# Load order and first row tiles of a layernorm + attention + SwiGLU kernel: weight pieces issued ahead of x, and transposes split over two PSUM banks

## The chip, the cores and the metric

The kernel runs on one core of one Trainium2 chip. The metric is the time of one execution on the device, in microseconds (us). Executions of one kernel mostly differ by 0.8 to 1.8 us; so single executions are read through their profiles, of which there is one per run, and times only as medians and means of five or more.

The engines are TensorE (PE in the profile), VectorE (DVE), ScalarE (ACT), GpSimd (POOL) and SyncE (SP, which here issues most transfers). "SPq" is the sequencer of SyncE.

## The reference, cut to what matters

```python
x  = A_x                                   # 2048 x 640, bf16
xn = layernorm(x)                          # over the 640 columns
s  = attention(xn @ wq, last 512 of K and V, 32 heads of 192) @ wo
g  = silu((silu(xn @ w_gate) * (xn @ w_up)) @ w_down)     # hidden width 1536
return x + s * g
```

The kernel starts with the FFN. For that it needs the normalised x transposed (640 as five blocks of 128 partitions, `xnT`) and the weights w_gate and w_up. Only the first 512 rows, four tiles of 128 rows that are called tile 0 to tile 3 here, and their x that is called x0 to x3, are in the reach of the change.

## The kernel before: the parts that matter

The loads are issued in program order. The first quarter of the columns of each weight comes in three pieces: block 0, blocks 1 and 2, blocks 3 and 4 ("first", "second" and "third piece").

```python
load_x(0)                                   # two halves: SyncE and ACT
load_x(1, nc.scalar)
for cs in (slice(0, 1), slice(1, 3), slice(3, NC)):      # NC = 5 blocks
    if cs.stop == NC:
        load_x(2)
    for eng, w_sb, w in ((nc.sync, wg_sb, B_w_gate), (nc.scalar, wu_sb, B_w_up)):
        ...
        eng.dma_start(out=w_sb[:, cs, 0:FQ], in_=src)
load_x(3)
```

Each tile goes through statistics (DVE), a Sqrt (ACT), reciprocal and normalisation (DVE), five transposes into PSUM (TensorE), a copy to `xnT` (ACT; for tile 0 ACT and DVE) and 30 matmuls of 128 columns (TensorE). The next tile is prepared in the middle of the current one:

```python
for t in range(4):
    order = [(*fs, [c]) for c in range(NC) for fs in banks]   # block by block
    if t:
        order = [(*fs, range(NC)) for fs in banks]            # all five blocks at once
    for k, (f, s, cs) in enumerate(order):
        if k == len(order) * 3 // 5 and t < 3:
            if t == 1:
                ln_stats(3, lambda: ln_apply(2))   # DVE: half of x3's statistics, then tile 2's normalisation
            else:
                ln_apply(t + 1)
            ready(t + 1)                           # transposes and copy of the next tile
            if t == 0:
                ln_stats(2)
            ...
        hidden_mm(first[f][s][:, rows], s, f, rows, cs)
```

After these four tiles the FFN goes on with matmuls of 512 columns. "The start of the 512-wide matmuls" is therefore the moment at which the start-up is over.

The softmax here doesn't subtract the row's maximum and nothing guards it: scores larger than these inputs give would overflow.

Of the kernel before, what the change touches and what calls it, by code (L numbers as in the profile page):

```python
# [15 lines left out]
def kernel(  # L16
# [13 lines left out]
    nc = tc.nc  # L30
    P = nc.NUM_PARTITIONS

    x2 = A_x.flatten_outer_dims()
# [9 lines left out]
    NC = D // P  # L43
# [27 lines left out]
    def sc_tile():  # L71
        return psum.tile([P, 2, 512], f32, name="sc", tag="sc")

    def mm_tile():
        return psum.tile([P, 2, 512], f32, name="mm", tag="mm")
# [4 lines left out]
    xnT = res.tile([P, NC, Sq], bf, name="xnT")  # L80
# [3 lines left out]
    ident = consts.tile([P, P], bf, name="ident")  # L84
# [62 lines left out]
    lo, hi = slice(0, 64), slice(64, 128)  # L147
# [17 lines left out]
    with ExitStack() as fctx:  # L165
# [6 lines left out]
        zero_t = ffw.tile([P, 512], bf, name="zero_t")  # L172
        nc.vector.memset(zero_t[:], 0.0)
        wg_sb = ffw.tile([P, NC, F], bf, name="wg_sb")
        wu_sb = ffw.tile([P, NC, F], bf, name="wu_sb")
        wd_sb = ffw.tile([P, NF, D], bf, name="wd_sb")
        FQ = F // 4
        x_t, ln, xns = {}, {}, {}

        def load_x(t, eng=nc.sync):  # L180
            x_t[t] = lnx.tile([P, D], bf, name="x_t")
            if t == 0:
                for r, eng in ((lo, nc.sync), (hi, nc.scalar)):
                    eng.dma_start(out=x_t[t][r, :], in_=x2[t * P + r.start : t * P + r.stop, :])
            else:
                eng.dma_start(out=x_t[t][:], in_=x2[t * P : (t + 1) * P, :])

        def load_gu(q):
            cols = slice(q * FQ, (q + 1) * FQ)
            nc.sync.dma_start(  # L190
                out=wg_sb[:, :, cols], in_=B_w_gate[:, cols].rearrange("(c p) f -> p c f", p=P)
            )
            nc.sync.dma_start(
                out=wu_sb[:, :, cols], in_=B_w_up[:, cols].rearrange("(c p) f -> p c f", p=P)
            )

        load_x(0)
        load_x(1, nc.scalar)
        for cs in (slice(0, 1), slice(1, 3), slice(3, NC)):
            if cs.stop == NC:  # L200
                load_x(2)
            for eng, w_sb, w in ((nc.sync, wg_sb, B_w_gate), (nc.scalar, wu_sb, B_w_up)):
                src = w[cs.start * P : cs.stop * P, 0:FQ].rearrange("(c p) f -> p c f", p=P)
                eng.dma_start(out=w_sb[:, cs, 0:FQ], in_=src)
        load_x(3)
        load_gu(1)
        for t in range(4, 8):
# [6 lines left out]
        nc.scalar.activation(act_t[:], one_t[:], ACT.Sqrt)  # L214
        warm = sc_tile()

        def keep_warm(n):
            for _ in range(n):
                nc.tensor.matmul(warm[:, 0, :], zero_t[:, 0:P], zero_t[:], start=True, stop=True)

        keep_warm(11)

        def ln_stats(t, between=None):
            b, ti = divmod(t, 4)
            if ti == 0:
                ln[b] = [lnw.tile([P, 4, 2], f32, name="mv"), lnw.tile([P, 4], f32, name="rstd")]
            stats = lnw.tile([P, ng, nc.vector.BN_STATS_DIM], f32, name="stats")
            for g in range(ng):
                nc.vector.bn_stats(stats[:, g, :], x_t[t][:, g * (D // ng) : (g + 1) * (D // ng)])
                if g == 0 and between:  # L230
                    between()
            nc.vector.bn_aggr(ln[b][0][:, ti, :], stats[:])
# [7 lines left out]
        def ln_sqrt(t):  # L240
            mv, rstd = ln[0]
            nc.scalar.activation(
                rstd[:, t : t + 1], mv[:, t, 1:2], ACT.Sqrt, bias=eps_t[:], scale=1.0
            )

        def ln_apply(t, parts=(slice(0, D),)):
            b, ti = divmod(t, 4)
            mv, rstd = ln[b]
            xns[t] = lnx.tile([P, D], bf, name="xn", bufs=4)
            if b == 0:  # L250
                nc.vector.reciprocal(rstd[:, t : t + 1], rstd[:, t : t + 1])
            for cols in parts:
                nc.vector.tensor_scalar(
                    xns[t][:, cols], x_t[t][:, cols], mv[:, ti, 0:1], rstd[:, ti : ti + 1],
                    op0=ALU.subtract, op1=ALU.mult,
                )

        tps = {}

        def ln_transpose(t):  # L260
            xn = xns.pop(t)
            tps[t] = tp[:, t % 2, 0 : NC * P].rearrange("p (c k) -> p c k", c=NC)
            for c in range(NC):
                nc.tensor.transpose(tps[t][:, c, :], xn[:, c * P : (c + 1) * P], ident[:])

        def ln_transpose_dma(t):
            nc.sync.dma_start_transpose(
# [5 lines left out]
        def hidden_mm(out, s, f, qc, cs=range(NC)):  # L273
            w_sb = (wg_sb, wu_sb)[s]
            for c in cs:
                nc.tensor.matmul(  # L276
                    out, w_sb[:, c, f * P : (f + 1) * P], xnT[:, c, qc],
                    start=(c == 0), stop=(c == NC - 1),
                )

        def hidden_gate(b, f, g, u):
            sg = ffa.tile([P, 512], bf, name="sg")
            nc.scalar.activation(sg[:], g, ACT.Silu)  # L283
            nc.vector.tensor_tensor(hTs[b][:, f, :], u, sg[:], ALU.mult)  # L284
# [35 lines left out]
        first = {f: [sc[:, s, :] for s in range(2)] for f, sc in ((0, sc_tile()), (1, sc_tile()))}  # L320
        tp = psum.tile([P, 2, 1024], bf, name="tp", tag="mm")
        first[2] = [mm[:, s, :] for mm in (mm_tile(),) for s in range(2)]
        def ready(t):
            ln_transpose(t)
            rows = slice(t * P, (t + 1) * P)
            n = NC if t else 2
            nc.scalar.copy(xnT[:, 0:n, rows], tps[t][:, 0:n, :])
            if n < NC:
                nc.vector.tensor_copy(out=xnT[:, n:NC, rows], in_=tps[t][:, n:NC, :])

        ln_stats(0)
        ln_sqrt(0)
        ln_stats(1, lambda: ln_apply(0, (slice(0, 2 * P), slice(2 * P, D))))
        ready(0)
        ln_sqrt(1)
        keep_warm(3)
        banks = [(f, s) for f in range(3) for s in range(2)]
        for t in range(4):
            rows = slice(t * P, (t + 1) * P)

            order = [(*fs, [c]) for c in range(NC) for fs in banks]
            if t:
                order = [(*fs, range(NC)) for fs in banks]
            for k, (f, s, cs) in enumerate(order):
                if k == len(order) * 3 // 5 and t < 3:
                    if t == 1:
                        ln_stats(3, lambda: ln_apply(2))
                    else:
                        ln_apply(t + 1)
                    ready(t + 1)  # L350
                    if t == 0:
                        ln_stats(2)
                    if t < 2:
                        ln_sqrt(t + 2)
                    else:
                        nc.scalar.activation(act_t[:], one_t[:], ACT.Silu)
                hidden_mm(first[f][s][:, rows], s, f, rows, cs)
                if t == 3 and s == 1:
                    hidden_gate(0, f, *first[f])
# [394 lines left out]
```

## Time and profile before

| | before |
|---|---|
| median of 6 executions | 927.25 us (926.93 to 928.28) |
| span of the profiled execution | 925.4 us |
| first real matmul | 6.89 us |
| statistics of x2 start (DVE) | 8.09 us |
| transposes of tile 2 start (TensorE) | 10.55 us |
| 512-wide matmuls start | 15.56 us |

The page's first part gives for each engine its busy time, its share of the span and its instructions:

```profile
PE 917.3 (99%) x11085; PEld 624.9 (68%) x11101; DVE 575.6 (62%) x844; ACT 473.8 (51%) x847; POOL 100.1 (11%) x387
```

TensorE is busy for all but 8 us of the span, and part of these 8 us lies in the start, which is why a change there has so little to win. The last two rows of the table come from the timeline of TensorE (start, duration, line, operation, output and input, shapes, count):

```profile
10.55 0.45 PE L264 MATMUL tp<-ident,xn 128*128 128x128 bf16 x5
...
15.56 1.24 PE L276 MATMUL mm<-xnT,wg_sb 128*128 128x512 bf16 x4
```

The transposes of tile 2 have no idle time noted: before, tile 2 came just in time.

### The profile page before, as it was taken

To read this page: it belongs to the slowest core of one execution; us is meant where nothing else is said; L and a number is where in the kernel's file an instruction comes from. 1 tells how busy PE (TensorE), PEld (TensorE's weight loads), DVE (VectorE), ACT (ScalarE), POOL (GpSimd) and SP (SyncE) were. 2 spreads that over 40 slices of the span, in tenths; PEclk is the share of its full clock that TensorE was granted. 3 is DMA by queue.
4 is the path that set the end of the run, shared out by engine and by line. 5 is a ranking of instruction groups with operands and counts; after the bars stand their busy time and mean duration, and the time that the engine had idled before them with its cause. 6 is when DMAs were issued, how large, how long until landed. Compare 5 with 4: busy or idle time off the path is not lost.

```text
span 925.4 us, 25770 instructions
## 1 busy us (share of the span) xinstructions
PE 917.3 (99%) x11085; PEld 624.9 (68%) x11101; DVE 575.6 (62%) x844; ACT 473.8 (51%) x847; POOL 100.1 (11%) x387
## 2 busy tenths in 40 slices
PE   9999999999999999999999999999999999999997
PEld 5455556575858585868686867676767777776665
DVE  6433331467676767676766667676767676767655
ACT  4222222556464646565555565656555555556561
POOL 0000000000000000000000000000000000002976
PEclk9999999999999999999999999999999999999999
DMA  9321510044544445444536262536362717162624
GB/s 298 72 56 33 114 35 1 1 77 89 87 79 83 83 80 86 75 90 70 95 60 106 59 107 55 111 53 113 46 119 42 124 36 129 36 129 76 135 57 140
DMA packets 243810, 77.18 MB, mean 83 GB/s; under 512 B 224624, under 2 KB 243696, under 8 KB 243696
## 3 DMA queue, kind: packets, MB, share of 16 engines
q1 hardware_dynamic: 242640, 74.72, 41.5%
q8 instruction: 87, 1.43, 0.7%
q10 hardware_dynamic: 1056, 0.82, 0.3%
q14 instruction: 27, 0.22, 0.1%
HBM read 39.45 MB, written 2.62 MB: 45 GB/s over the span
## 4 chain that ended last, share of the span: by engine, by line
PE 98%; DMA 1%; DVE 0%; issue 0%; ACT 0%; DVEq 0%
PE mm L428 22%; PE sc L563 19%; PE sc L442 18%; PE mm L468 16%; PE sc L276 11%; PE mm L298 6%; PE sc L537 3%; PE mm L520 2%; DMA wg_sb<-in_B_w_gate_dram 1%; PE mm L276 0%; PE mm L311 0%; DMA OT_b<-O_b 0%; PE sc L520 0%; DMA x_t<-in_A_x_dram 0%; DVE s_f L638 0%
## 5 line engine op out<-in xcount | busy, mean ns | idle before, releaser
L446 ACT ACTIVATE p_t<-sc 128x1024 bf16<-128x1024 f32 x254 | 253.0, 1022 | 130.5 <-PE sc L442 130.5
L433 DVE TENSOR_REDUCE qT<-mm 128x512 bf16<-128x1024 f32 x189 | 231.2, 1223 | 104.8 <-PE mm L428 102.4
L498 ACT ACTIVATE O_b<-mm,r 128x192 bf16<-128x192 f32 x486 | 164.6, 421 | 183.1 <-issue 159.9
L428 PE MATMUL mm<-xnT,wq_p 64*128 64x512 bf16 x1890 | 237.7, 377 | 0.0
L563 PE MATMUL sc<-wo_p,OT_b 64*128 64x320 bf16 x2592 | 217.4, 296 | 0.5 <-DMA OT_b<-O_b 0.5
L588 DVE TENSOR_TENSOR sacc<-sacc,sc 128x640 f32<-128x640 f32 x200 | 164.1, 821 | 78.3 <-PE sc L563 78.3
L442 PE MATMUL sc<-qT,khat 64*128 64x512 bf16 x1524 | 198.3, 377 | 0.0
L468 PE MATMUL mm<-V_p,p_t 64*128 64x193 bf16 x3520 | 186.4, 243 | 0.0
L468 PEld LDWEIGHTS <-p_t 64*128 64x128 bf16 x3584 | 162.6, 94 | 12.0
L428 PEld LDWEIGHTS <-wq_p 64*128 64x128 bf16 x1890 | 105.6, 94 | 96.0 <-issue 0.5
L563 PEld LDWEIGHTS <-OT_b 64*128 64x128 bf16 x2592 | 139.9, 94 | 22.7 <-DMA OT_b<-O_b 1.1
L442 PEld LDWEIGHTS <-khat 64*128 64x128 bf16 x1536 | 85.6, 94 | 79.2 <-issue 2.9
L551 POOL MEMSET turn_t<- 128x1 f32 x328 | 32.2, 98 | 697.9 <-PE mm L468 474.6
L284 DVE TENSOR_TENSOR hT<-sc,sg 128x512 bf16<-128x512 f32 x46 | 31.7, 690 | 85.2 <-ACT sg L283 85.1
L283 ACT ACTIVATE sg<-sc 128x512 bf16<-128x512 f32 x46 | 27.3, 596 | 72.4 <-PE sc L276 72.4
L276 PE MATMUL sc<-xnT,wg_sb 128*128 128x512 bf16 (+1 forms) x248 | 58.6, 354 | 1.0 <-DMA wg_sb<-in_B_w_gate_dram 0.4
L276 PE MATMUL sc<-xnT,wu_sb 128*128 128x512 bf16 (+1 forms) x259 | 59.1, 355 | 0.1
L298 PE MATMUL mm<-wd_sb,hT 128*128 128x320 bf16 x384 | 56.6, 300 | 0.0
L487 DVE RECIPROCAL r<-mm 128x4 f32<-128x4 f32 x124 | 22.7, 183 | 48.1 <-PE mm L468 36.3
L298 PEld LDWEIGHTS <-hT 128*128 128x128 bf16 x384 | 37.5, 98 | 18.9
L276 PEld LDWEIGHTS <-wu_sb 128*128 128x128 bf16 x285 | 26.3, 98 | 26.9
L276 PEld LDWEIGHTS <-wg_sb 128*128 128x128 bf16 x285 | 26.3, 98 | 23.5 <-DMA wg_sb<-in_B_w_gate_dram 0.5
(67 smaller groups left out, 373.1 us busy)
## 6 DMA issues: line engine op xcount, KB each, us to landing
wo_p<-in_A_wo_dram SPq DMA_DIRECT2D x16, 480.0 KB, 4.6
K_p<-in_A_k_cache_dram SPq DMA_DIRECT2D x32, 192.0 KB, 3.4
V_p<-in_A_v_cache_dram SPq DMA_DIRECT2D x32, 192.0 KB, 3.0
wq_p<-in_A_wq_dram SPq DMA_DIRECT2D x64, 80.0 KB, 3.1
wq_p<-in_A_wq_dram SPq DMA_DIRECT2D x16, 160.0 KB, 3.5
x_r<-in_A_x_dram SPq DMA_DIRECT2D x16, 160.0 KB, 3.9
x_t<-in_A_x_dram SPq DMA_DIRECT2D x14, 160.0 KB, 3.0
OT_b<-O_b SPq DMA_TRANSPOSE x124, 2.8
```

Source lines behind the costliest of these rows:

```text
L276: nc.tensor.matmul(out, w_sb[:, c, f * P : (f + 1) * P], xnT[:, c, qc], start=(c == 0), stop=(c == NC - 1),)
L284: nc.vector.tensor_tensor(hTs[b][:, f, :], u, sg[:], ALU.mult)
L298: nc.tensor.matmul(dn[:, 0:HD], hTs[b][:, f, ti * P : (ti + 1) * P], wd_sb[:, f, cols], start=(f == 0), stop=(f == NF - 1),)
L428: nc.tensor.matmul(q_ps[:, h, :], pairs[pr]["wq"][r, c, j * P : (j + 1) * P], xnT[r, c, b * 512 : (b + 1) * 512], start=(c == 0), stop=(c ...
L433: nc.vector.reduce_sum(qTs[i][:, j, :], q_ps[:, :, :].rearrange("p h n -> p n h"), axis=AX.X)
L442: nc.tensor.matmul(sc[:, h, :], khat[r, j, ks], qT[r, j, :], start=(j == 0), stop=(j == 2))
L446: nc.scalar.activation(p_t[:, :, :], sc[:, :, :], ACT.Exp, scale=scale)
L468: m = nc.tensor.matmul(acc[:, k, h * 256 : h * 256 + Dh + 1], Ps[i][kc][r, h, qt * P : (qt + 1) * P], V_p[r, kc, h, 0 : Dh + 1], start=(p ...
L498: nc.scalar.activation(O_b[:, qt, h, :], a_k[:, h, 0:Dh], ACT.Copy, scale=r[:, k, h, :])
L551: st["turn"] = nc.gpsimd.memset(turn_t[:], 0.0)
L563: m = nc.tensor.matmul(ps[:, n, 0:HD], OTs[i][r, 3 * qt + j, :], pairs[i // NB]["wo"][r, j, n * HD : (n + 1) * HD], start=(turn == 0 and j ...
L588: nc.vector.tensor_tensor(s_t, s_t, sc[:, :, 0:HD], ALU.add)
```

## The change

Its intent: tile 0 needs the weight pieces soon and x1 and x2 later, so the pieces should go ahead. ACT should issue fewer transfers, so that its Sqrt table is loaded before it is needed. Transposes into two banks should let a copy begin while the other bank is still written. The warm-up matmuls, which only keep TensorE's clock up, should not delay the transposes.

```diff
         load_x(0)
-        load_x(1, nc.scalar)
-        for cs in (slice(0, 1), slice(1, 3), slice(3, NC)):
-            if cs.stop == NC:
-                load_x(2)
-            for eng, w_sb, w in ((nc.sync, wg_sb, B_w_gate), (nc.scalar, wu_sb, B_w_up)):
+        for n, cs in enumerate((slice(0, 1), slice(1, 3), slice(3, NC))):
+            for w_sb, w in ((wg_sb, B_w_gate), (wu_sb, B_w_up)):
+                eng = nc.scalar if n == 0 and w is B_w_up else nc.sync
                 ...
                 eng.dma_start(out=w_sb[:, cs, 0:FQ], in_=src)
+            if n == 0:
+                load_x(1)
+        load_x(2)
         load_x(3)
...
-        keep_warm(11)                       # 512 columns each
+        keep_warm(9)
+        keep_warm(3, P)                     # 128 columns each
...
+        PARTS = (slice(0, 2), slice(2, NC))
+        def ready(t):
+            ...                             # part[n]: bank n of tp, blocks PARTS[n]
+            for n, cs in enumerate(PARTS):
+                for k, c in enumerate(range(cs.start, cs.stop)):
+                    nc.tensor.transpose(part[n][:, k, :], xn[:, c * P : (c + 1) * P], ident[:])
+            for n, cs in enumerate(PARTS):
+                if n and t == 0:
+                    nc.vector.tensor_copy(out=xnT[:, cs, rows], in_=part[n])
+                else:
+                    nc.scalar.copy(xnT[:, cs, rows], part[n])
...
-        keep_warm(3)
+        keep_warm(3, P)
...
-            if t:                           # tiles 1 to 3 took all five blocks at once
+            if t == 3:                      # now only tile 3 does
                 order = [(*fs, range(NC)) for fs in banks]
```

More of the change, by code (lines that the diff above doesn't have):

```diff
@@ L178, with load_x @@
         x_t, ln, xns = {}, {}, {}
-        def load_x(t, eng=nc.sync):
+        def load_x(t):
             x_t[t] = lnx.tile([P, D], bf, name="x_t")
-            if t == 0:
-                for r, eng in ((lo, nc.sync), (hi, nc.scalar)):
-                    eng.dma_start(out=x_t[t][r, :], in_=x2[t * P + r.start : t * P + r.stop, :])
-            else:
-                eng.dma_start(out=x_t[t][:], in_=x2[t * P : (t + 1) * P, :])
+            for r, eng in ((lo, nc.sync), (hi, nc.scalar)) if t == 0 else ((slice(0, P), nc.sync),):
+                eng.dma_start(out=x_t[t][r, :], in_=x2[t * P + r.start : t * P + r.stop, :])
         def load_gu(q):
@@ L215, with keep_warm @@
         warm = sc_tile()
-        def keep_warm(n):
+        def keep_warm(n, cols=512):
             for _ in range(n):
-                nc.tensor.matmul(warm[:, 0, :], zero_t[:, 0:P], zero_t[:], start=True, stop=True)
-        keep_warm(11)
+                nc.tensor.matmul(warm[:, 0, 0:cols], zero_t[:, 0:P], zero_t[:, 0:cols], start=True, stop=True)
+        keep_warm(9)
+        keep_warm(3, P)
         def ln_stats(t, between=None):
@@ L256, in ln_apply @@
                 )
-        tps = {}
-        def ln_transpose(t):
-            xn = xns.pop(t)
-            tps[t] = tp[:, t % 2, 0 : NC * P].rearrange("p (c k) -> p c k", c=NC)
-            for c in range(NC):
-                nc.tensor.transpose(tps[t][:, c, :], xn[:, c * P : (c + 1) * P], ident[:])
+        PARTS = (slice(0, 2), slice(2, NC))
+        def ready(t):
+            xn, rows = xns.pop(t), slice(t * P, (t + 1) * P)
+            part = [tp[:, n, 0 : (cs.stop - cs.start) * P].rearrange("p (c k) -> p c k", k=P)
+                    for n, cs in enumerate(PARTS)]
+            for n, cs in enumerate(PARTS):
[6 more added lines that the diff above has]
+                    nc.scalar.copy(xnT[:, cs, rows], part[n])
         def ln_transpose_dma(t):
@@ L322 @@
         first[2] = [mm[:, s, :] for mm in (mm_tile(),) for s in range(2)]
-        def ready(t):
-            ln_transpose(t)
-            rows = slice(t * P, (t + 1) * P)
-            n = NC if t else 2
-            nc.scalar.copy(xnT[:, 0:n, rows], tps[t][:, 0:n, :])
-            if n < NC:
-                nc.vector.tensor_copy(out=xnT[:, n:NC, rows], in_=tps[t][:, n:NC, :])
         ln_stats(0)
```

## The prediction

> **What bounds the kernel now.** I read the page's shares and its chain first, then one table of windows over the start, then the chain of the first 20 us, and last the timelines of DVE and ACT there. The page's chain says that TensorE ends last:
>
> ```profile
> PE 98%; DMA 1%; DVE 0%; issue 0%; ACT 0%; DVEq 0%
> ```
>
> The table of windows (columns: stretch, its length, then busy time and instruction count of each engine, clock, DMA share, GB/s) cuts the span where the diff cuts it:
>
> ```profile
> 1.23:5.86 4.63, 4.63 (x12) 1.58 (x12) 2.11 (x7) 1.67 (x3) 0.16 (x3) 1.00 0.73 210
> 5.86:6.89 1.03, 1.03 (x9) 0.57 (x9) 0.80 (x4) 0.45 (x2) 0.00 (x0) 1.00 0.97 320
> 6.89:9.01 2.12, 1.75 (x24) 1.35 (x22) 1.72 (x6) 0.45 (x2) 0.00 (x0) 1.00 1.04 347
> 9.01:11.78 2.77, 2.77 (x48) 2.68 (x48) 1.82 (x6) 1.30 (x4) 0.00 (x0) 1.00 1.09 350
> 11.78:15.94 4.16, 4.16 (x68) 3.86 (x67) 0.68 (x3) 2.90 (x6) 0.00 (x0) 1.00 1.09 335
> 15.94:925.40 909.46, 902.99 (x10931) 614.83 (x10944) 568.14 (x819) 467.02 (x834) 99.35 (x379) 1.00 0.42 80
> ```
>
> After 15.94 us TensorE is busy 902.99 of 909.46 us, and the diff touches nothing there. All that it can move is the moment at which the first four row tiles are through (15.56 us, where the 512-wide matmuls begin); a shift there passes to the end one for one. The first real matmul starts at 6.89 us, so even a perfect start gains a few us of 927, under 1%. The chain of the first 20 us (start, duration, what) names the waits:
>
> ```profile
> 0.72 2.80 DMA x_t<-in_A_x_dram
> ...
> 3.53 5.44 DMA wg_sb<-in_B_w_gate_dram
> 8.97 0.05 issue
> 9.01 0.40 PE sc L276 x4
> ```
>
> The third piece of w_gate, issued at 3.53, lands at 8.97, and TensorE stands about 0.5 us before 9.01. That is the wait the change aims at. The row tiles have a second chain, in the timeline of DVE (start, duration, line, operation, then the idle time before it and what ended it):
>
> ```profile
> 4.66 0.44 DVE L229 BATCH_NORM_STATS2 stats<-x_t 128x6 f32<-128x320 bf16 x1
> 5.17 0.16 DVE L251 RECIPROCAL rstd<-rstd 128x1 f32<-128x1 f32 x1
> ...
> 6.85 0.36 DVE L329 COPY xnT<-tp 128x384 bf16<-128x384 bf16 x1 [0.19 <-ACT xnT L327]
> ...
> 8.09 0.89 DVE L229 BATCH_NORM_STATS2 stats<-x_t 128x6 f32<-128x320 bf16 x2 [0.33 <-DMA x_t<-in_A_x_dram]
> 9.01 0.21 DVE L232 BATCH_NORM_AGGREGATE mv<-stats 128x2 f32<-128x12 f32 x1
> 9.45 0.49 DVE L229 BATCH_NORM_STATS2 stats<-x_t 128x6 f32<-128x320 bf16 x1 [0.23 <-DMA x_t<-in_A_x_dram]
> 9.86 0.15 DVE L251 RECIPROCAL rstd<-rstd 128x1 f32<-128x1 f32 x1
> 10.04 0.45 DVE L253 TENSOR_SCALAR xn<-x_t,mv,rstd 128x640 bf16<-128x640 bf16 x1
> ```
>
> DVE waits for x's third tile (index 2) until 8.09 and for the fourth until 9.45. The normalised tile 2 is done at 10.49, and TensorE transposes it at 10.54, just when it has run out of other work. So the arrival of x is as tight as that of the weights. The ACT timeline gives the rest:
>
> ```profile
> 3.46 1.28 ACT L214 ACT_TABLE_LOAD   x1 [3.46 <-DMA x_t<-in_A_x_dram]
> 4.75 0.20 ACT L214 ACTIVATE act_t<-one_t 128x1 f32<-128x1 f32 x1
> 4.86 0.28 ACT L242 ACTIVATE rstd<-mv,eps_t 128x1 f32<-128x1 f32 x1
> 6.44 0.37 ACT L327 COPY xnT<-tp 128x256 bf16<-128x256 bf16 x1 [1.30 <-PE tp L264]
> ```
>
> **What the Trainium skill says.** "ScalarE: Activation LUTs", section "What ACT_TABLE_LOAD costs", gives about 1283 ns for the load; this trace has 1.28 us. "PSUM — Partial Sum Buffer", section "PSUM bank collisions raise a hardware error", says that two engines must not access one bank at once, even at different columns; here DVE's copy of tile 0 starts only once ACT's copy of the same bank has ended, 0.19 us of it idle. "DMA: Bandwidth & Descriptors", section "Issuing engines are not separate DMA queues", says that issuing from a second engine saves only issue time; the trace has five issues on ACT between 0.72 and 3.43 us, and the transfers together move 250 to 350 GB/s after that. "TensorE: Matmul & The Clock Gate", Part 1, says that the clock is at half until about 3.4 us of sustained activity in a free-running window; the trace's eleven 512-wide warm-ups start 0.43 us apart and the 128-wide matmuls after 6.89 only 0.055 us apart, which agrees.
>
> **The change, part by part.**
>
> Table load. ACT now issues two transfers instead of five, so the load starts near 1.95 and ends near 3.2, not 4.74. But tile 0's statistics are ready only at 4.75, and the Sqrt started at 4.86: the gain is the 0.1 us of the dummy Sqrt in between, at most.
>
> Two banks, two copies. For tile 0 the intent is that ACT copies the first two blocks while three are still being transposed, and DVE copies beside it. The built program does not do that. TensorE signals once, at the last of the five transposes, and ACT's first copy waits for that signal, as before; DVE's copy still waits for ACT's copy. So tile 0 gains nothing: 0.0 us. For tiles 1 to 3 one copy of 0.69 us becomes two. From the rows of 256 columns (0.37) and 640 (0.69) a column costs 0.83 ns with 0.16 us fixed, so the halves take 0.37 and 0.48, about 0.06 us more in all if they overlap by 0.1, and this sits on ACT ahead of the next Sqrt. In exchange the next tile may start 0.3 us sooner; TensorE waited about 0.12 us for the copy ahead of tile 2 and again ahead of tile 3. Tile 3 keeps the order that needs all five blocks at once and waits for the second half. Net: 0.0 to -0.1.
>
> Warm-ups. Nine long and three short in place of eleven end near 5.4 instead of 6.0, but the transposes waited for DVE until 5.77 anyway: 0.0. The three after the transposes shrink from 0.21 us to 0.05 each; they ended when the copy ended: 0.0.
>
> Order of loads. I count bytes ahead of a piece and take the landing of the transfer that had as many ahead of it before. Before, x0 80+80 KB, x1 160, the first pieces 2 x 96, the second 2 x 192, x2 160, the third 2 x 192, x3 160: 1600 KB, and landings (issue plus time to landing) of 4.4 for x1, 4.7 and 4.9 for the first pieces, 7.3 and 7.5 for the second, 8.1 for x2, 8.4 and 8.97 for the third, 9.4 for x3. After, nearly all is on one queue: x0, first pieces, x1, second, third, x2, x3. x1 has 512 KB up to its end: near 4.9 instead of 4.4. Second pieces 704 and 896 KB: 6.1 and 7.4. Third 1088 and 1280: 7.9 and 8.5. x2 1440: 8.9 instead of 8.1. x3 1600: 9.4 as before.
>
> The effects of that. DVE runs in order and has x1's first statistics (0.44) ahead of tile 0's reciprocal, so tile 0 moves by 4.9 + 0.44 - 5.10, some 0.25 later: first matmul at 7.1. The second pieces then cost no wait, the third a mere 0.1, and tile 0 ends near 9.2 instead of 9.70: **-0.5 us**. Tile 1 does 18 of its 30 matmuls (1.0 us) and TensorE wants to transpose tile 2 at 10.2. But tile 2 needs, from x2's landing, 0.89 of statistics, 0.21 aggregate, 0.3 Sqrt with hand-over, half of tile 3's statistics in between, reciprocal and 0.45 apply: 2.2 us in all. From 8.9 that is 11.1, against 10.54: **+0.6 us**, which replaces the gain. From there tiles 2 and 3 take as long as before.
>
> Sum: +0.5 us if transfers go at the former rate. If a single queue moves the bytes faster (the rate between 4 and 5 us was 216 GB/s, later 350), every landing comes earlier; with 0.5 us earlier, the sum is near 0.0, and with 1.0 us it is limited by TensorE's own work, -0.3. I give the three 0.15, 0.40 and 0.45, because one queue alone kept 350 GB/s from 8 us on: 0.15 x 0.5 + 0.40 x 0.0 - 0.45 x 0.3 = -0.06, so 927.31 - 0.06, **927.2 us**.
>
> **The rivals.** First, the gain is whole: x2 lands by 8.0, tile 2 is ready at 10.2, TensorE no longer stands, and the time falls by 0.4 to 0.9, to 926.4 to 926.9. For it speaks the slow stretch at 4 to 5 us while both queues had work; against it, the unchanged byte count up to x3. Second, x's third tile becomes the wait in place of the third weight piece, +0.3 to +0.8, 927.6 to 928.1. For it speaks that DVE already waits 0.33 us for x2 at 8.09. Third, the clock: the shorter warm-ups leave TensorE idle from 5.4 to about 5.8 and mostly from 6.3 to 7.1. If a free-running window then counts as idle, matmuls run at half speed for up to 3.4 us more, some +0.5 to +1.5 in some executions. Against it, over two thirds of such a window are still busy.
>
> **Range and chances.** The three runs before spread by 1.35 us, more than the effect, so the range is the mechanisms' span with that noise: 926.3 to 928.3. Two per cent would be 18.5 us, more than the whole start; same is nearly certain: faster 0.005, same 0.99, slower 0.005.
>
> **What would show it.** In the profile after: the Sqrt table load at about 2 us; tile 0's ACT copy still after all five transposes and DVE's copy after it; no wait for w_gate at 9 us; x1's statistics starting later than 4.66 and x2's later than 8.09; a gap on TensorE ahead of the transposes of tile 2, ended by DVE's apply; and 512-wide matmuls beginning between 15.2 and 16.1. I am wrong if x2 lands by 8.1 although it is issued last, if DVE's copy runs beside ACT's, if matmuls of tile 0 stand 0.107 us apart, or if anything after 16 us differs by more than the shift.

## The result, and the profile after

| | before | after |
|---|---|---|
| median of 6 executions | 927.25 us | 928.38 us |
| lowest to highest | 926.93 to 928.28 | 928.01 to 928.90 |
| span of the profiled execution | 925.4 us | 926.1 us |

The ratio is 1.0011 (95% interval 0.9998 to 1.0024): the same at the 2% level. Ratios here are the mean time of one kernel's fast runs over the mean of the other's of the same rounds, so they are not quite the ratio of the medians. This interval contains 1, so these twelve executions alone do not set "slower" apart from "equal"; e6 below repeats the measurement. The changed kernel is 1.1 us slower in the median, and its profiled execution, which was the fastest of the six, has a span 0.7 us longer.

The page's chain now shows the transfer of x where the one of a weight piece stood, and in the first 20 us of the chain (start, duration, what) it reads:

```profile
4.20 0.47 SPq L199
4.71 4.43 DMA x_t<-in_A_x_dram
...
9.17 0.90 DVE stats L228 x2
...
10.86 0.46 DVE xn L252
11.36 0.47 PE tp L266 x5
```

SyncE issues the last weight piece until 4.7 us, only then x2, and x2 lands 4.43 us later at 9.14. Its statistics, its normalisation and its transposes follow without a pause worth the name. The timeline of DVE says the same with its waits (in brackets: the idle time before, and what ended it):

```profile
5.30 0.49 DVE L228 BATCH_NORM_STATS2 stats<-x_t 128x6 f32<-128x320 bf16 x1 [0.64 <-DMA x_t<-in_A_x_dram]
...
7.37 0.36 DVE L269 COPY xnT<-tp 128x384 bf16<-128x384 bf16 x1 [0.19 <-ACT xnT L271]
...
9.17 0.89 DVE L228 BATCH_NORM_STATS2 stats<-x_t 128x6 f32<-128x320 bf16 x2 [0.89 <-DMA x_t<-in_A_x_dram]
```

x1's statistics start at 5.30 instead of 4.66, x2's at 9.17 instead of 8.09. The middle line shows the two banks of tile 0: DVE's copy still stands 0.19 us until ACT's copy is done, exactly as before. ACT's timeline shows the table load moved up as intended, and its first copy still released by the transposes:

```profile
1.95 1.28 ACT L212 ACT_TABLE_LOAD   x1 [1.95 <-issue]
3.24 0.20 ACT L212 ACTIVATE act_t<-one_t 128x1 f32<-128x1 f32 x1
...
6.97 0.37 ACT L271 COPY xnT<-tp 128x256 bf16<-128x256 bf16 x1 [1.97 <-PE tp L266]
```

On TensorE, tile 0 is through at about 9.4 us instead of 9.7 (block 4's last matmuls), because the wait for the third piece of w_gate is nearly gone. Then it stands ahead of tile 2:

```profile
11.36 0.45 PE L266 MATMUL tp<-ident,xn 128*128 128x128 bf16 x5 [0.76 <-DVE xn L252]
...
16.39 0.81 PE L283 MATMUL mm<-xnT,wg_sb 128*128 128x512 bf16 x3
```

The transposes of tile 2 are 0.81 us later than before and the 512-wide matmuls 0.83 us later; from one to the other it took 5.03 us, against 5.01 before. The table of windows, with the columns and stretches of the one shown of before, says where the transfers lost:

```profile
5.86:6.89 1.03, 0.59 (x8) 0.42 (x9) 0.99 (x3) 0.00 (x0) 0.00 (x0) 1.00 0.86 196
6.89:9.01 2.12, 1.83 (x32) 1.62 (x30) 1.12 (x5) 0.70 (x3) 0.00 (x0) 1.00 0.87 285
9.01:11.78 2.77, 2.01 (x37) 1.84 (x35) 2.50 (x8) 0.91 (x3) 0.00 (x0) 1.00 0.96 290
11.78:15.94 4.16, 4.05 (x70) 3.76 (x68) 0.78 (x3) 2.84 (x6) 0.00 (x0) 1.00 1.08 354
15.94:926.10 910.16, 904.58 (x10958) 614.60 (x10955) 568.08 (x819) 467.94 (x837) 99.34 (x379) 1.00 0.42 80
```

Between 5.86 and 9.01 us the rate is 196 and 285 GB/s where it was 320 and 347; only from 11.78 us on is it as high as before (354). Over these 3.15 us that is some 0.26 MB less moved (1.03 x 124 + 2.12 x 62, in KB), at a moment when x2, one of the last in the row, is waited for. TensorE's 2.01 of 2.77 us between 9.01 and 11.78 hold the gap ahead of tile 2. From the start of the 512-wide matmuls to the end of the span it is 909.7 us after and 909.8 before: the start-up's loss reaches the end one for one, and nothing else was gained or lost there.

### The profile page after: what moved, and what is told of

It reads as the page before. It is cut to its first block, busy times and chain, and to the rows that moved or that the text cites. A ratio compares the mean times of both kernels' runs of the same rounds, so it can differ in the third digit from the quotient of the medians.

```text
span 926.1 us, 25792 instructions
## 1 busy us (share of the span) xinstructions
PE 917.4 (99%) x11102; PEld 623.8 (67%) x11102; DVE 575.5 (62%) x844; ACT 474.2 (51%) x850; POOL 100.1 (11%) x387
## 4 chain that ended last, share of the span: by engine, by line
PE 97%; DMA 1%; DVE 1%; SPq 0%; ACT 0%; issue 0%; DVEq 0%
PE mm L427 22%; PE sc L562 19%; PE sc L441 18%; PE mm L467 16%; PE sc L283 10%; PE mm L305 6%; PE sc L536 3%; PE mm L519 2%; DMA x_t<-in_A_x_dram 0%; PE mm L318 0%; PE sc L519 0%; DMA OT_b<-O_b 0%; PE mm L283 0%; SPq L199 0%; DVE s_f L637 0%
## 5 line engine op out<-in xcount | busy, mean ns | idle before, releaser
L283 PE MATMUL sc<-xnT,wg_sb 128*128 128x512 bf16 (+1 forms) x260 | 60.7, 354 | 0.4 <-ACT xnT L271 0.3
```

What stands on the lines that cost most here:

```text
L283: nc.tensor.matmul(out, w_sb[:, c, f * P : (f + 1) * P], xnT[:, c, qc], start=(c == 0), stop=(c == NC - 1),)
```

## The experiments

Theory A: x2, issued behind the weight pieces, lands later, and tile 2 waits for it. The rivals: the other parts of the change cost the time (two copies, order of the tiles, warm-ups); the issue from one engine does; x1's delay does; or TensorE's clock stays at half through tile 0 because of the shorter warm-ups. The texts call the theories by letters, of which A is always the one above; B is the other parts in e1 and e2 and a gain without a late tile 2 in e5, C is x1's delay in e3 and e4 and the clock from e9 on. All times are medians with the mean behind the stroke. All outputs are right. The kernel before, run in the same calls, had 927.37 / 927.33 in the first call (the first four kernels), 927.16 / 927.22 in the second (the next four) and 927.36 / 927.43 in the third. The three calls ran on three different chips, and the profile of before is that of the first measurement, so tenths of a microsecond between profiles of different calls are not to be trusted. The 95% interval of the ratio to before lies above 1 in e6 (1.0001 to 1.0025), e7 (1.0022 to 1.0050) and e11 (1.0001 to 1.0028); in all the others it contains 1.

The profiles of all of them in one table (us; start of x2's statistics, of tile 2's transposes and of the 512-wide matmuls):

| kernel | x2 | tile 2 | 512-wide | time, median / mean |
|---|---|---|---|---|
| before | 8.09 | 10.55 | 15.56 | 927.25 / 927.40 |
| after | 9.17 | 11.36 | 16.39 | 928.38 / 928.43 |
| e1, new load order alone | 8.67 | 10.86 | 15.88 | 927.71 / 927.83 |
| e2, all but the load order | 8.05 | 10.75 | 15.76 | 927.51 / 927.71 |
| e3, after, x2 ahead of the third pieces | 8.04 | 10.52 | 15.53 | 927.79 / 927.96 |
| e4, after, x1 early from ACT | 8.50 | 10.69 | 15.72 | 927.27 / 927.53 |
| e5, before, x2 behind the third pieces | 8.95 | 11.14 | 16.16 | 928.33 / 928.16 |
| e6, after, unchanged | 8.94 | 12.16 | 17.19 | 928.47 / 928.39 |
| e7, after, x2 behind x3, x4, x5 | 10.24 | 12.44 | 17.46 | 929.59 / 930.50 |
| e8, e3 with later waits mended | 8.10 | 10.70 | 15.28 | 927.16 / 927.32 |
| e9, after with long warm-ups | 9.16 | 11.35 | 16.38 | 928.10 / 928.19 |
| e10, e8 with long warm-ups | 8.13 | 10.84 | 15.42 | 927.78 / 927.95 |
| e11, before, 5 long warm-ups | 7.82 | 11.71 | 16.73 | 928.66 / 928.63 |
| e12, before, after's warm-ups | 7.82 | 10.32 | 15.33 | 927.19 / 927.47 |

### e1: the new load order alone

The loads of the changed kernel in the kernel before, nothing else:

```diff
-        load_x(1, nc.scalar)
         ...
-            if cs.stop == NC:
-                load_x(2)
+            if n == 0:
+                load_x(1)
+        load_x(2)
```

> The kernel before with nothing but the new order of loads (x's second tile after the first weight pieces, its third after the last, all later issues on SyncE; the Sqrt table load moves up with it). Theory A, x's third tile comes later and DVE is too late with tile 2: x2's statistics start near 9.2 instead of 8.09, the transposes of tile 2 start near 11.3 instead of 10.54, the 512-wide matmuls near 16.4 instead of 15.56, the time is 0.7 to 1.0 us over before, as in the whole change. Rival B, the loss comes from the copies, the order of matmuls or the warm-ups: the 512-wide matmuls start at 15.6 or earlier and the time is within 0.3 us of before.

In the timelines of DVE and TensorE:

```profile
8.67 0.89 DVE L227 BATCH_NORM_STATS2 stats<-x_t 128x6 f32<-128x320 bf16 x2 [0.31 <-DMA x_t<-in_A_x_dram]
...
15.88 1.24 PE L274 MATMUL mm<-xnT,wg_sb 128*128 128x512 bf16 x5
```

The direction was as expected, the size was not: in this execution x2 landed at 8.65, not at 9.14, and the loss is 0.32 us. From x2's statistics to tile 2's transposes it is 2.19 us, as after, and then 5.02. The load order alone makes a loss as large as the landing is late; the same order of loads may land half a microsecond earlier.

### e2: everything but the load order

The changed kernel with the old loads (the reverse of e1's edit).

> The changed kernel with the old order of loads put back; two banks, two copies, the order of matmuls in tiles 1 and 2 and the short warm-ups stay. Theory A: x2's statistics start at 8.1 again; tile 2's transposes start near 10.7, because 18 matmuls instead of 15 stand ahead of them; the 512-wide matmuls start at 15.6 to 15.8; the time is 0.0 to +0.3 us against before. Rival B: most of the +0.8 us stays, the 512-wide matmuls start near 16.3.

x2 is back at 8.05, and 0.2 us of loss remain (15.76). They come on TensorE, as the trace reads (no run changes the order alone): tile 1 now goes block by block, so 18 instead of 15 matmuls stand ahead of tile 2's transposes, and the next Sqrt waits behind two copies on ACT. This is a cost of the other parts when x2 is in time. It does not add to the 0.83: where x2 is late, TensorE has time for three more matmuls while it waits. One of the five executions took 929.54 us; the profile, of another one, does not show why.

### e3: x2 ahead of the third pieces

```diff
-        load_x(2)
+            if n == 1:
+                load_x(2)
```

> The changed kernel with one load moved: x's third tile is issued ahead of the third weight pieces, as before the change. Theory A: it lands near 8.1 to 8.5 instead of 9.14, the gap on TensorE ahead of the transposes of tile 2 (0.9 us) shrinks to under 0.4; the third pieces land some 0.5 later and cost up to 0.5 us in tile 0; the 512-wide matmuls start at 15.7 to 16.1 instead of 16.39. Rival C, the late second tile (statistics at 5.30 instead of 4.66) is what costs: no change, 16.3 to 16.5.

```profile
8.04 0.88 DVE L229 BATCH_NORM_STATS2 stats<-x_t 128x6 f32<-128x320 bf16 x2
...
15.53 1.24 PE L284 MATMUL mm<-xnT,wg_sb 128*128 128x512 bf16 x5
```

One moved load in the changed kernel brings x2 back to 8.04 and the 512-wide matmuls to 15.53, as early as before and better than expected, with everything else of the change, x1 behind the first pieces too, in place. The rival that expected 16.3 or more falls. The wait for the third pieces is back in exchange (0.38 us from the start of one matmul to that of the next, 8.51 to 8.89). The time did not show it clearly: 927.79, between both kernels, with two of five executions over 928.5.

### e4: x1 early again

```diff
+        load_x(1, nc.scalar)
         for n, cs in enumerate(...):
             ...
-            if n == 0:
-                load_x(1)
```

> The changed kernel with x's second tile issued from ScalarE right behind the first, as before the change; all else as changed. Theory A: the first real matmul comes at 6.9 to 7.0 instead of 7.39 and tile 0 ends up to 0.4 earlier, but x2 still lands near 9.1, so the gap ahead of tile 2's transposes grows by what tile 0 gained and the 512-wide matmuls start at 16.2 to 16.4 as in the changed kernel. Rival C: they start 0.4 to 0.6 us earlier, at 15.8 to 16.0, and the time falls as much.

Tile 0 began at 6.80 instead of 7.39, so x1's place does set tile 0. I had expected x2 to stay at 9.1 and the end of the start-up with it; x2 landed at 8.5, so that number was missed, and the 512-wide matmuls at 15.72 and the median of 927.27, 1.1 us under after's, look like what the rival had forecast. The run does not decide by these numbers: with one issue fewer on SyncE, x2 was issued at 4.23 instead of 4.71, so both x1 and x2 moved. What speaks for theory A in the trace is that TensorE's gap ahead of tile 2 did not shrink with the earlier tile 0 (0.78 us of idle time, against 0.76) and that the 512-wide matmuls followed x2: 8.50 + 2.19 + 5.03 = 15.72. The half microsecond won in tile 0 went into the wait for tile 2. The runs that move one of the two alone are e3 (x1 late, x2 early: no loss at 15.53) and e5.

### e5: only x2 moved, in the kernel before

```diff
-            if cs.stop == NC:
-                load_x(2)
             ...
+        load_x(2)
         load_x(3)
```

> The kernel before with one load moved: x's third tile is issued behind the third weight pieces, as in the change; both issuing engines as before. Theory A: it lands at 8.5 to 9.1 instead of 8.06, tile 2's transposes start about 2.2 us after that, at 10.7 to 11.3 instead of 10.54, the third pieces land earlier, so tile 0 ends before 9.5, and the 512-wide matmuls start at 15.7 to 16.3. Rival B: only tile 0 gets faster, the 512-wide matmuls start at 15.1 to 15.4 and the time falls by 0.3.

```profile
8.95 0.89 DVE L228 BATCH_NORM_STATS2 stats<-x_t 128x6 f32<-128x320 bf16 x2 [0.95 <-DMA x_t<-in_A_x_dram]
...
16.16 1.24 PE L275 MATMUL mm<-xnT,wg_sb 128*128 128x512 bf16 x4
```

Here ACT and SyncE still share the issuing and x1 is still early, but x2 is late and the loss is +0.60 in the profile, +1.2 in the median and +0.9 in the mean. So the place of x2 in the row is enough; one issuing engine is not needed for it.

### e6: the changed kernel once more

> The changed kernel again, unaltered, as a control: the first run of its load order in the kernel before had x2 land at 8.65 where the changed kernel had 9.14, so the landing varies from execution to execution. Theory A: x2 lands between 8.5 and 9.3 here too; whatever the landing L is, the transposes of tile 2 start at L + 2.2 (within 0.1) and the 512-wide matmuls 5.0 later (within 0.15); the time is 0.3 to 1.1 us over before. If the start of the 512-wide matmuls doesn't follow the landing, theory A falls.

The time is that of the first measurement. The profile is not: x2 landed at 8.92, but tile 2's transposes came 3.22 us after its statistics instead of 2.19. The 512-wide matmuls did not follow the landing, so by its own words theory A fell in this execution, which was the slowest of the five (928.91). The timelines of TensorE and DVE say why:

```profile
8.21 0.31 PE L283 MATMUL mm<-xnT,wg_sb 128*128 128x128 bf16 x1
8.31 0.31 PE L283 MATMUL mm<-xnT,wu_sb 128*128 128x128 bf16 x1
...
11.46 0.16 DVE L250 RECIPROCAL rstd<-rstd 128x1 f32<-128x1 f32 x1 [1.03 <-ACT rstd L241]
...
12.16 0.45 PE L266 MATMUL tp<-ident,xn 128*128 128x128 bf16 x5
```

The matmuls of tile 0 start 0.107 us apart, twice the 0.055 of all other profiles before this one; from 10.4 us on they are 0.055 apart again. So the matmuls ran at half rate through tile 0 (the clock column of `--windows` says 1.00 there all the same, so the spacing is the only sign). Tile 1's transposes then came late (9.70 us), ACT's copies of tile 1 behind them, the Sqrt of tile 2 behind the copies (11.12), and DVE stood 1.03 us for that Sqrt. TensorE itself was through with its matmuls only at about 12.0. Two delays meet here, and this time x2 was not the later one. What is left of theory A is that x2 sets the time where the matmuls of tile 0 run at full rate.

### e7: x2 later still

```diff
-        load_x(2)
-        load_x(3)
+        for t in (3, 4, 5, 2):
+            load_x(t)
```

> The changed kernel with x's third tile issued behind three more tiles of x (480 KB more ahead of it): a larger dose of the suspected cause. Theory A: it lands 1.2 to 1.6 us later than in the changed kernel of this call, and tile 2's transposes, the 512-wide matmuls and the time move by the same 1.2 to 1.6 us. Theory in which the late tile is hidden by other work: a shift of under 0.5 us.

```profile
10.24 0.89 DVE L228 BATCH_NORM_STATS2 stats<-x_t 128x6 f32<-128x320 bf16 x2 [1.78 <-DMA x_t<-in_A_x_dram]
```

x2's statistics are 1.07 us later than after, and so are the 512-wide matmuls (17.46 against 16.39); the median is 1.1 us above e6's. The dose follows. The increase is a little under the expected 1.2 to 1.6. Those were meant against e6: there the statistics moved by 1.30, as expected, but tile 2's transposes only by 0.28, because e6's profile has the half rate. Two of the six executions were at 931.02 and 934.13, for which the one profile, of an execution at 929.27, shows no cause.

### e8: a version that should gain

From e3, with two later waits mended: Sqrt of tile 3 between the two copies of tile 2, and tile 3 also block by block, so that it does not wait for its second copy.

```diff
-                    ready(t + 1)
+                    ready(t + 1, (lambda: ln_sqrt(3)) if t == 1 else None)
...
-            if t == 3:
-                order = [(*fs, range(NC)) for fs in banks]
```

> A candidate. The changed kernel with x's third tile ahead of the third weight pieces, the Sqrt of tile 3 between the two copies of tile 2 instead of behind them, and tile 3 in the order of tiles 1 and 2, so that it doesn't need the second copy at its third matmul. Theory A adds up: tile 2's transposes at 10.5 as in the run with that load moved, tile 3's transposes 1.95 later instead of 2.16 because TensorE's own work sets them, no 0.28 us gap in tile 3: the 512-wide matmuls start at 15.0 to 15.2 and the time is 0.3 to 0.5 us under before. If the copies or the matmul order of tile 3 cost nothing, 15.5 and no gain.

The 512-wide matmuls start at 15.28, 0.28 us ahead of the kernel before and just above what was expected. The time, 927.16 / 927.32, against 927.16 / 927.22 of the kernel before, does not show it, and the forecast of 0.3 to 0.5 us under before was missed: a quarter of a microsecond cannot be told at this spread.

### e9 and e10: the long warm-ups back

In the changed kernel (e9) and in e8 (e10):

```diff
-        keep_warm(9)
-        keep_warm(3, P)
+        keep_warm(11)
...
-        keep_warm(3, P)
+        keep_warm(3)
```

> The changed kernel with the long warm-ups of before put back (eleven 512-wide at the start, three after the first transposes). Theory A+C: the late third tile costs 0.6 to 0.9 us in every execution, and the short warm-ups a further 0.8 to 1.2 us in about a third of them, because TensorE then stays at half clock through tile 0, as in the control run. So here no execution is cold: the matmuls of tile 0 are 0.055 us apart, no time is over 928.5, and the mean is 0.2 to 0.6 us under the changed kernel's 928.4, that is 0.5 to 0.9 over before. Theory A alone: the mean stays at 928.3 to 928.5.

> The candidate with the long warm-ups. Theory A+C: the 512-wide matmuls start at 15.1 to 15.4 in the profile as without them, the one slow execution of the candidate (928.36) has no counterpart, and the mean is 0.1 to 0.4 us under before, at 926.8 to 927.1. If the warm-ups don't matter, mean and spread stay as in the candidate, 927.3 and 1.5.

These asked how much of the changed kernel's time is the clock seen in e6. e9's profile is that of after (x2 at 9.16, 16.38), so the late x2 does not hang on the warm-ups. Its mean is 0.2 us under the two of the changed kernel, within the noise, and one of its executions took 929.03, where none over 928.5 had been expected. e10 missed too: 927.95 in the mean and one execution at 929.03, where 926.8 to 927.1 and no slow one had been expected; its 512-wide matmuls started at 15.42. So neither shows that the warm-ups matter to the mean, and no version here beats the kernel before in time.

### e11 and e12: the warm-ups alone, in the kernel before

```diff
-        keep_warm(11)
+        keep_warm(5)            # e11
...
-        keep_warm(11)
+        keep_warm(9)            # e12, and 128 columns for the last three, as after
+        keep_warm(3, P)
```

> The kernel before with five long warm-ups instead of eleven: TensorE stops near 3.4 us and stands until 5.8. A large dose of the suspected cause, everything else untouched. Theory C: no window of 3.4 us is busy enough before some 8.5 us, so every execution runs tile 0 at half clock: matmuls 0.107 us apart, the 512-wide matmuls start at 16.2 to 17.3 instead of 15.56, and the time rises by 0.6 to 1.7 us. If warm-ups did nothing: 15.5 and the time of before.

> The kernel before with only the warm-ups of the change (nine long and three short, then three short). Theory C: TensorE stands for 0.3 us before the first transposes and some 0.3 after, less than in the changed kernel where x's second tile comes late, so fewer executions go cold: the lowest time is that of before within 0.2, and none to two of five are over 928.2. Mean 0.0 to 0.4 over before. If the warm-ups did nothing: mean within 0.15 of before.

In e11 the half rate was made on purpose (the window of 3.4 us in its expectation is the one that the prediction takes from the skill; full rate shows only after 9.5 us, not from 8.5 on):

```profile
8.06 0.31 PE L276 MATMUL mm<-xnT,wg_sb 128*128 128x128 bf16 x1
8.17 0.31 PE L276 MATMUL mm<-xnT,wu_sb 128*128 128x128 bf16 x1
```

x2 was early (7.82), yet the 512-wide matmuls started at 16.73, +1.17, and the mean is +1.2. So a second cause exists, and where it strikes it can cost as much as the late x2 (+1.17 here against +0.83). With the change's own warm-ups in the kernel before (e12) the profiled execution has tile 0 at 0.055 us and the mean is that of the kernel before; one of five took 928.51. Both of its forecasts allow this, so e12 does not tell them apart.

## Why the prediction was right or wrong, point by point

The class, the same within 2%, was right, but that was safe: 2% would be 18.5 us, more than the whole start. The number was not right: 927.2 was predicted, 928.38 measured, 0.08 us above the top of the range, and slower instead of a shade faster. It is the second rival that came true, x's third tile in place of the third weight piece; its mechanism and its law were stated rightly, its size was a little low (+0.3 to +0.8), and the weight given to it was too small.

- **Table load.** As predicted: at 1.95 us and worth next to nothing, since the Sqrt waits for the statistics.
- **Two banks.** As predicted: in tile 0 DVE's copy waits 0.19 us for ACT's as before. The built program keeps its waits for the whole PSUM tile `tp`, whichever bank of it is used (read from who waits for whom; no run splits the tile).
- **Two copies for tiles 1 to 3, and the order of the tiles.** Predicted 0.0 to -0.1; after shows +0.02 (5.03 against 5.01 from tile 2's transposes on), and e2 shows +0.2 where x2 is in time. The step had counted copies and left out that three more matmuls stand ahead of tile 2's transposes.
- **Warm-ups.** Predicted 0.0, with the half clock as the third rival in some executions. e12 agrees with 0.0 in the mean; e6 shows that such an execution exists. The argument against it was that over two thirds of a window stay busy. They did, and it did not help: the stretch of 3.41 us before e6's tile 0, placed as the last section says, has 2.41 us of busy TensorE, transposes counted, 71%, and tile 0 ran at half rate all the same.
- **Landings.** Counted by bytes ahead at the former rate: x1 4.9, x2 8.9. The trace has x1 at 5.28 and x2 at 9.14, both later, x1 by most. The count's direction was right and its rate too high; e5, with two issuing engines, had x2 at 8.92. (One step left its own rule: the third piece of w_gate, with 1088 KB, belongs after the 8.1 that 1056 KB had before, not at 7.9.) (x3 no longer tells: its statistics wait for DVE, not for its landing.)
- **Tile 0's gain.** Predicted -0.5, measured about -0.3 (9.4 against 9.7), because x1 held tile 0 back to 7.39 instead of 7.1. Either way it is worth nothing while tile 2 waits (e4).
- **Tile 2.** "2.2 us in all" from x2's landing was measured as 2.19 to 2.20 from the start of x2's statistics in after, e1, e4, e5, e7 and e9. It does not hold where x2 is early: in before, e2, e3, e8, e10 and e12 it was 2.46 to 2.71, because DVE then waited for x3 or TensorE was not through. With x2's statistics at 9.17 that gives 11.36, +0.81 instead of +0.6.
- **The step that failed: the weighing.** The sum was +0.5 "if transfers go at the former rate" (tile 2's +0.6 less the 0.0 to 0.1 of the copies), and I gave that 0.15 and 0.85 to a row that moves faster, because one queue had kept 350 GB/s from 8 us on. The transfers went slower, 196 and 285 GB/s instead of 320 and 347 up to 9.01 us. The term of +0.5 measured +0.83 (+0.81 and +0.02), and nothing was set against it. The reading at fault is the comparison of rates at different times: a late rate was taken for an early one. After the change, too, the rate is 290 GB/s up to 11.78 us and 354 only from there on. (Nor did the transfers of the kernel before move 250 to 350 GB/s all the time after 3.43 us, as the prediction's paragraph on the skill says: by its own figure it was 216 between 4 and 5 us.)

**What is shown, and what is open.** Shown: a late x2 makes tile 2 late by what follows from its landing (after, e5, e7, and e3 as the reversal), and that makes the profiled execution late by nearly as much (in all of these profiles 909.6 to 910.0 us remain after the start of the 512-wide matmuls). Not shown is why the row moves fewer bytes between 5 and 9 us. The kept traces have a pattern (`--windows 5:9`): the five kernels in which ACT issues the pieces of w_up too (before, e2, e5, e11, e12) move 316 to 346 GB/s, the nine in which SyncE issues nearly all of them move 265 to 299. What the prediction takes from the skill, that a second issuing engine saves only issue time, would not lead one to expect this; but no run changes the issuing engine alone. x2 landed between 8.65 and 9.14 under the same loads (e1, after, e6, e9) and at 8.92 with two issuing engines (e5), so one execution of each does not tell the engine's part. The medians moved by 1.1 to 1.3 us (after and e6), more than the 0.7 (span) to 0.8 (start-up) of after's profile. The half rate of e6 may make up the rest, but how many executions of the changed kernel have it I did not measure, and e9 does not confirm it.

## What to carry to other kernels

Moving a load forward moves the others back: before reordering a row of loads, name for each transfer the work that waits for it and how much follows from its landing to the path (here 2.2 us for x2, which holds while x3, half of whose statistics stand in between, is no later), and compare these deadlines, not the waits one sees. Of two delays that meet at one instruction the later counts, so what was won in tile 0 was lost in the wait for x2. A split over two banks gains only if the built program waits for each bank by itself; look at the signal before counting the gain.

## What the Trainium skill lacked or had wrong

- "TensorE: Matmul & The Clock Gate", Part 1, names sustained activity of about 3.4 us but not how busy such a stretch has to be. In e6 the 3.41 us from 3.61 to 7.02 had TensorE busy for 2.41 us (71%, transposes counted), and the matmuls that followed stayed 0.107 us apart until 10.4 us. The place of that stretch is an estimate from the page's window: two times 3.41 us back from 10.43. In e1 the 3.41 us up to 4.31, where the weight loads of the warm-ups cease to be 0.43 us apart, had 3.08 us (90%), and full rate followed. A pause alone does not decide: TensorE stood 1.09 us ahead of the first transposes in e1 and 1.00 us in e6.
- "ScalarE: Activation LUTs", "What ACT_TABLE_LOAD costs", adds a drain of about 1.38 us to each switch of tables. Here the load took 1.28 us and the next ACTIVATE started 0.01 us after it, before and after the change; no drain of that size shows at this first load, nor at the second one of after, which starts at 14.80, 0.02 us after a copy ends, and is followed by an ACTIVATE at 16.09.
- No page that I read says that two banks of one PSUM tile are still one object for the waits of the built program: DVE's copy of the second bank stood 0.19 us for ACT's copy of the first.
- No page that I read says how far a landing varies from execution to execution: the same row of loads brought x2 at 8.65 to 9.14 us, as much as most of the gains sought here.
